# An RWKV block followed by a mixture of experts: the second product's weights copied into a tile with adjacent columns, the last routing groups reordered, row reads on two queues

## The chip, the core and the metric

The kernel runs on one core of a Trainium2 chip. A core has five engines that run side by side and meet through semaphores: TensorE (PE in the profile, its weight loads are PEld), VectorE (DVE), ScalarE (ACT), GpSimd (POOL) and SyncE (SP, which here only issues transfers). The metric is the device time of one execution in microseconds; lower is better. All data is float32.

## The reference, cut to what matters

```python
# attention: r, k, v of shape (4 batches, 8 heads, 768 steps, 48), decay w and bonus u per head
for t in range(S):
    cur  = einsum('bhd,bhe->bhde', u * k[t], v[t])
    y[t] = einsum('bhd,bhde->bhe', r[t], state + cur)
    state = w * state + einsum('bhd,bhe->bhde', k[t], v[t])
x = y rearranged to (3072 tokens, 384)

# mixture of experts: 4 groups x 4 experts, D = 384, F = 1024
g_idx = argmax(x @ w_group);            g_w = softmax(...)[g_idx]
e_idx = argmax(x @ w_expert[g_idx]);    e_w = softmax(...)[e_idx]
out[token] = g_w * e_w * (relu(x @ w1[g, e]) @ w2[g, e])
```

Each token goes to one of 16 experts. The two products `x @ w1` (384 by 1024) and `h @ w2` (1024 by 384) are the bulk of the arithmetic of the second half.

## The kernel before

The attention part works in chunks of 128 steps. As the tokens of a group of tiles are done, they are routed: logits, the choice of expert, a place in that expert's region of a buffer in device memory (`x_sorted`), and an indirect transfer (a scatter) that writes each row to its place. Then 17 items are worked through in turn. Items 0 and 1 both belong to the expert that is picked first (128 rows each); items 2 to 16 are one expert each, with 240, 233, 222, 216, 212, 206, 202, 199, 196, 193, 190, 187, 184, 178 and 173 rows.

```python
SLOTS = [256, 240, 233, 222, 216, 212, 206, 202, 199, 196, 193, 190, 187, 184, 178, 173]
ITEMS = [(0, 0, P), (0, P, SLOTS[0])] + [(e, 0, SLOTS[e]) for e in range(1, GE)]

# two places for an expert's weights, used in turn
places = [
    (wpool.tile([P, KO, F], FP32, name="w1"), wpool.tile([P, FO, DM], FP32, name="w2")),
    (kall..., rall...),            # the attention's tiles, used again
]

def up(i, f, beside=None):         # first product, two of eight blocks of 128 of F
    ...
    for q in range(2):
        if q == 1 and beside is not None:
            beside()
        for ko in range(KO):       # KO = 3
            nc.tensor.matmul(ph[:, q, :], lhsT=w1[:, ko, P * (f + q) : P * (f + q + 1)], rhs=xe[:, ko, 0:w], ...)
    nc.scalar.activation(hTs[i][:, f : f + 2, 0:w], ph, AF.Relu)

def down(i, d, beside=None):       # second product, one of three blocks d
    ...
    for fo in range(FO):           # FO = 8
        nc.tensor.matmul(
            po, lhsT=w2[:, fo].rearrange("p (c k) -> p k c", k=KO)[:, d], rhs=hT[:, fo, 0:w], ...
        )
    nc.scalar.copy(yo[i][:, d, 0:w], po)
```

A block `d` of the second product takes columns d, d + 3, d + 6, ... of `w2`: its weights lie 12 bytes apart in the tile. The rows come in with four transfers and a small one for the keys, are transposed by VectorE (`columns`), and leave by `pieces_out`: transposes, a multiplication by the gate, and scatters to the output.

```python
LAST = 5
for s in range(NT + LAST):         # NT = 24 tiles
    ...
    if s == FOUR * B + 10:         # s = 26
        columns(0)
    ...
    # rows_T(s - 4), row_logits(s - 5), back(s - 3), values(s - 2), scores(s - 1)
    if n in ROUTED:                # n = s - 5; the last groups are n = 21 and n = 23, two tiles each
        choice, before, gate, place, rows = routing(n)
        ...
    if s == FOUR * B + 10:
        up(0, 0)
up(0, 2)
placing = [part for _, part in todo.pop(NT + LAST)]
up(0, 4, placing[0])               # before() of the last group, between the two halves
for part in placing[1:]:           # gate(), place(), the scatters
    part()
up(0, 6)
load_rows(1, first, nc.sync)
... down(0, 0) ... down(0, 1); down(0, 2)
load_rows(2, second, nc.sync)
weights[1] = load_expert(second, 1)
...
columns(1)
pieces_out(0)
for i in range(1, len(ITEMS)):
    up(i, 0); up(i, 2)
    if i > 1: pieces_out(i - 1)
    up(i, 4); up(i, 6)
    if e < GE: load_rows(i + 2, expert, nc.sync)       # e = this expert + 2
    down(i, 0); columns(i + 1); down(i, 1); down(i, 2)
    if e < GE: weights[e] = load_expert(expert, e % 2)
```

Of the kernel before, what the change touches and what calls it, by code (L numbers as in the profile page):

```python
# [8 lines left out]
FP32 = mybir.dt.float32  # L9
# [25 lines left out]
def kernel(  # L35
# [313 lines left out]
    def route(pool, rb, xt, T, sums, number, group, apart=False):  # L349

        def tl(shape, name, dtype=FP32):
            return pool.tile(shape, dtype, tag=f"{name}_{T}", name=name)

        taken = [0]

        def part(k, pattern, **sizes):
            a = taken[0]  # L360
            taken[0] += T * k
            return rb[:, a : a + T * k].rearrange(pattern, i=T, **sizes)

        L = part(NL, "p (i a e) -> p i a e", e=Eg)
        key = part(NL, "p (i a e) -> p i a e", e=Eg)
        ohx = part(GE, "p (i g e) -> p i g e", e=Eg)
        ohp = part(GE, "p (i g e) -> p i g e", e=Eg)
        sx = part(NA, "p (i a) -> p i a")
        se = part(1, "p (i a) -> p i a")
        ohg = tl([P, T, Eg], "ohg")  # L370
        place_f = part(1, "p (i a) -> p i a")
        pre = bank([P, T, GE], "pre") if apart else part(GE, "p (i e) -> p i e")
        mx, kx = tl([P, T, NA], "mx"), tl([P, T, NA], "kx")
        ohe = tl([P, T, G, Eg], "ohe")
        ex = tl([P, T, NA, Eg], "ex")
        place_i = tl([P, T], "place_i", U32)

        def choice():
            nc.vector.reduce_max(out=mx, in_=L, axis=AX)

            nc.vector.tensor_tensor(out=key, in0=L, in1=spread(mx, 3, Eg), op=OP.is_ge)
            nc.vector.tensor_mul(
                key.rearrange("p i a e -> p (i a) e"), key.rearrange("p i a e -> p (i a) e"), spread(desc, 1, T * NA)
            )
            nc.vector.reduce_max(out=kx, in_=key, axis=AX)
            nc.vector.tensor_tensor(out=ohg, in0=key[:, :, 0, :], in1=spread(kx[:, :, 0], 2, Eg), op=OP.is_equal)
            nc.vector.tensor_tensor(out=ohx, in0=key[:, :, 1:NA, :], in1=spread(kx[:, :, 1:NA], 3, Eg), op=OP.is_equal)
            nc.vector.tensor_mul(ohe, ohx, spread(ohg, 3, Eg))
            nc.vector.tensor_mul(ohp, ohx, spread(ohg, 3, Eg))
            for i in range(T):  # L390
                nc.vector.tensor_add(sums[:, i + 1, :], sums[:, i, :], ohp[:, i].rearrange("p g e -> p (g e)"))
            nc.vector.tensor_sub(ex, L, spread(mx, 3, Eg))
            nc.scalar.activation(ex, ex, AF.Exp)

        def before():
            nc.tensor.matmul(
                pre.rearrange("p i e -> p (i e)"), lhsT=later, rhs=ohe.rearrange("p i g e -> p (i g e)"),
                start=True, stop=False,
            )
            nc.tensor.matmul(  # L400
                pre.rearrange("p i e -> p (i e)"), lhsT=ones, rhs=sums[:, 0:T, :].rearrange("p i e -> p (i e)"),
                start=False, stop=True,
            )

        def gate():
            nc.vector.reduce_sum(out=sx, in_=ex, axis=AX)
            gg = tl([P, T, G], "gg")
            nc.vector.scalar_tensor_tensor(
                out=gg, in0=sx[:, :, 1:NA], scalar=1e-9, in1=ohg, op0=OP.add, op1=OP.mult
            )  # L410
            ge = tl([P, T, 1], "ge")
            nc.vector.reduce_sum(out=ge, in_=gg, axis=AX)
            nc.vector.scalar_tensor_tensor(out=se, in0=sx[:, :, 0:1], scalar=1e-9, in1=ge, op0=OP.add, op1=OP.mult)
            nc.vector.reciprocal(xt[:, :, DM + ROW_GATE : DM + ROW_GATE + 1], se)
            nc.scalar.copy(xt[:, :, DM + ROW_ID], number)

        def place():
            at = tl([P, T, GE], "at")
            nc.vector.tensor_mul(at, pre, ohe.rearrange("p i g e -> p i (g e)"))
            nc.vector.reduce_sum(out=place_f, in_=at, axis=AX)  # L420
            nc.vector.tensor_copy(place_i, place_f.rearrange("p i a -> p (i a)"))

        def rows(i):

            ins = nc.gpsimd.indirect_dma_start(  # L425
                out=xs_dram, out_offset=bass.IndirectOffsetOnAxis(ap=place_i[:, i : i + 1], axis=0),
                in_=xt[:, i, :], in_offset=None, bounds_check=GE * RG - 1, oob_is_err=False,
            )
            tc.declare_no_dep(ins.ins, group=group, reason="no place is given twice")
            tc.add_to_no_dep_group(group, ins.ins)  # L430

        return choice, before, gate, place, rows

    places = [
        (wpool.tile([P, KO, F], FP32, name="w1"), wpool.tile([P, FO, DM], FP32, name="w2")),
# [2 lines left out]
            rall.rearrange("p j a h d -> p (j a h d)")[:, 0 : FO * DM].rearrange("p (k d) -> p k d", d=DM),  # L438
        ),
    ]  # L440

    def load_w1(e, i):
        for q in range(P // BL):
# [44 lines left out]
    def padded(n):  # L488
        return -(-n // BL) * BL

    def load_rows(i, expert, queue):

# [6 lines left out]
        xg, key = xgs[i] = tl([P, n // BL, KO, BL], "xg"), tl([P, n // BL, ROW_EXTRA], "key")  # L501
        a, w, rows = ITEMS[i][1], padded(width(i)), regions[bass.ds(expert, 1)]
        for q in range(P // BL):
            queue.dma_start(
                out=xg[BL * q : BL * (q + 1), 0 : w // BL].rearrange("t b k d -> t b (k d)"),
                in_=rows[:, a : a + w, BL * KO * q : BL * KO * (q + 1)].rearrange("a (b t) d -> t (a b) d", t=BL),
            )
        p = P if is_last(i) else BL
        n = -(-w // p) * p
        queue.dma_start(out=key[0:p, 0 : n // p], in_=rows[:, a : a + n, DM:XW].rearrange("a (j p) w -> p (a j) w", p=p))  # L510

    def columns(i):
        xg, key = xgs.pop(i)
        w = padded(width(i))
        xe = xes[i] = item_tile(i, [P, KO, room(i)], "xe")
        for ko in range(KO):
            nc.vector.transpose(xe[:, ko, 0:w].rearrange("p (b t) -> p b t", t=BL), xg[:, 0 : w // BL, ko, :])  # L517
        ids = item_tile(i, [P, room(i) // BL], "ids", U32, bufs=4)
        gates = item_tile(i, [P, room(i) // BL], "gates", bufs=4)
        if is_last(i):  # L520
# [16 lines left out]
    def up(i, f, beside=None):  # L537
# [13 lines left out]
                )  # L551
        nc.scalar.activation(hTs[i][:, f : f + 2, 0:w], ph, AF.Relu)  # L552

    def down(i, d, beside=None):

        w = width(i)
        if d == 0:
            yo[i] = item_tile(i, [P, KO, room(i)], "yo")
            if w < padded(w):
                nc.vector.memset(yo[i][:, :, w : padded(w)], 0.0)  # L560
        w2, hT = weights[ITEMS[i][0]][1], hTs[i]
        po = bank([P, w], "po")
        for fo in range(FO):
            if fo == FO // 2 and beside is not None:
                beside()
            nc.tensor.matmul(  # L566
                po, lhsT=w2[:, fo].rearrange("p (c k) -> p k c", k=KO)[:, d], rhs=hT[:, fo, 0:w], start=(fo == 0), stop=(fo == FO - 1)
            )
        nc.scalar.copy(yo[i][:, d, 0:w], po)  # L569

# [180 lines left out]
    def routing(n):  # L751
# [3 lines left out]
        b0 = b + 1 - T  # L755
        return route(
            rpool, lgs.pop(n), xts[c][:, b0 : b + 1, :], T, cum[:, first : n + 2, :], tok[:, c, b0 : b + 1],
            "rows to places", n == NT - 1,
        )

    scale_k(0, nc.vector, 0, 1)
# [9 lines left out]
            skip_runtime_bounds_check_because="four bits of a whole number",  # L771
        )

    LAST = 5
    for s in range(NT + LAST):
        pieces = todo.pop(s, [])

# [32 lines left out]
        n = s - 5  # L810
        if 0 <= n < NT:
            row_logits(n)
        if 0 <= s - 3 < NT:
            back(s - 3)
        if 0 <= s - 2 < NT:
# [21 lines left out]
            span_decay()  # L837
        if s == 4:
            check_decay()
        if n in ROUTED:  # L840
            choice, before, gate, place, rows = routing(n)
            T = ROUTED[n]
            if n >= NT - B - 1:
                choice()
                todo.setdefault(s + 1, []).extend(
                    [("last", part) for part in (before, gate, place)]
                    + [("last", lambda i=i, rows=rows: rows(i)) for i in range(T)]
                )
            else:
                todo.setdefault(s + 1, []).append(("choice", choice))  # L850
                todo.setdefault(s + 2, []).extend([("first", before), ("last", gate), ("last", place)])
                for i in range(T):
                    at = s + 3 + (0 if n == FOUR * B - 1 else i)
                    todo.setdefault(at, []).append(("last", lambda i=i, rows=rows: rows(i)))
        if s == FOUR * B + 10:
            up(0, 0)
    up(0, 2)
    placing = [part for _, part in todo.pop(NT + LAST)]
    up(0, 4, placing[0])
    for part in placing[1:]:  # L860
        part()
    up(0, 6)
    load_rows(1, first, nc.sync)

    left_i = cst([1, 1], "left_i", I32)
    keys = token_keys(NT)
# [25 lines left out]

    with ExitStack() as moe:
        pools[1] = moe.enter_context(tc.tile_pool(name="moe", bufs=2, reuse_waits="tile"))
        with tc.manual_schedule(engines={mybir.EngineType.PE}):
            columns(1)
            pieces_out(0)
            for i in range(1, len(ITEMS)):
                up(i, 0)
                up(i, 2)  # L900
# [8 lines left out]
                down(i, 0)  # L909
                if i + 1 < len(ITEMS):  # L910
                    columns(i + 1)
                down(i, 1)
                if i + 1 < len(ITEMS):
                    down(i, 2)
# [6 lines left out]
    with tc.If(more > 0, preferred_fallthrough_block=False):  # L921
        with tc.tile_pool(name="rest", bufs=1) as rest:
# [15 lines left out]
            with tc.If(ok < 1):  # L938
                with tc.tile_pool(name="scan", bufs=1) as sc:
# [54 lines left out]
                    with tc.For_i(0, NT, 1) as i:  # L994
# [7 lines left out]
                        rb = route_bank()  # L1002
                        logits(xT, rb[:, 0:NL])
                        again = route(sc, rb, xr, 1, cum[:, 0:2, :], number, "rows to places again")
                        for part in again[0:4]:
                            part()
                        again[4](0)
                        nc.vector.tensor_copy(cum[:, 0, :], cum[:, 1, :])
                        nc.vector.tensor_scalar(out=number, in0=number, scalar1=float(P), scalar2=None, op0=OP.add)
                    nc.vector.tensor_copy(cum[:, NT, :], cum[:, 0, :])  # L1010
# [136 lines left out]
```

## Time and profile before

| | |
|---|---|
| median of 3 runs | 452.63 us (451.78 to 452.81) |
| span of the profiled execution | 450.0 us, mean granted TensorE clock 0.994 |
| attention, routing, first product of item 0 | 0 to 164.41 us |
| second product of item 0, all of item 1 (128 rows each) | 164.41 to 190.03 us |
| items 2 to 16 | 190.03 us to the end |

A row of a group of instructions reads: line, engine, operation, output and inputs, shapes, count, then busy microseconds, mean nanoseconds of one, and the engine's idle time before them with what ended it. A float32 matmul of the program is two matmul instructions in the trace, so the 24 matmuls of one `up` or `down` block are 48 records. The mean time of one matmul record contains its way through the array; how often one can start is read from the starts of blocks in the order of time. In a table of stretches the granted clock is 1.00 for full speed, and the DMA share is the mean busy share of the 16 transfer engines (values a little over 1 occur in short stretches).

### The profile page before, as it was taken

What the parts mean: (1) busy time and instruction counts of PE and PEld (TensorE: products, weight loads), DVE (VectorE), ACT (ScalarE), POOL (GpSimd) and SP (SyncE); (2) the same over time, 40 slices, a digit from 0 to 9 for tenths busy, and PEclk for the clock granted to TensorE, in tenths of its full rate; (3) what the DMA queues carried; (4) which work ended last, traced back from release to release, by engine and by line L of the source; (5) the groups of instructions that cost most, each with busy time, mean ns of one, the idle gap of its engine ahead of it and who ended that gap; (6) DMA issues with size and microseconds to landing.
All of it is one profiled execution on the core that took longest, in us unless ns stands there. A gap on an engine that the chain in (4) does not pass through costs nothing. (4 is left out here: it accounts for less than half of the span.)

```text
span 450.0 us, 9430 instructions
## 1 busy us (share of the span) xinstructions
PE 432.0 (96%) x3463; PEld 419.5 (93%) x3463; DVE 186.9 (42%) x616; ACT 138.6 (31%) x418; POOL 198.7 (44%) x209
## 2 busy tenths in 40 slices
PE   6899999999999798999999999999999999999994
PEld 5698999999999698999999999999999999999993
DVE  6575678867795862223031230132133232121111
ACT  2884565556556321121121211211211211111110
POOL 7855536666653243031533623623632632442351
PEclk9999999999999998999999999999999999999999
DMA  9999999970116646998987989899998998989200
GB/s 175 239 253 197 263 272 210 212 143 37 37 38 164 202 147 153 269 263 181 276 222 167 249 231 198 233 242 205 248 247 181 260 252 179 271 230 232 73 23 29
DMA packets 126418, 86.65 MB, mean 193 GB/s; under 512 B 98982, under 2 KB 115509, under 8 KB 126364
## 3 DMA queue, kind: packets, MB, share of 16 engines
q1 hardware_dynamic: 115020, 69.18, 67.1%
q0 software_dynamic: 4960, 9.48, 7.0%
q10 hardware_dynamic: 6384, 7.31, 5.0%
q8 instruction: 29, 0.48, 0.5%
q14 instruction: 25, 0.20, 0.2%
HBM read 70.15 MB, written 16.44 MB: 192 GB/s over the span
## 5 line engine op out<-in xcount | busy, mean ns | idle before, releaser
L605 POOL DMA_INDIRECT out_dram<-yp,ids x104 | 101.0, 972 | 168.3 <-DVE yo L560 125.3
L598 DVE STREAM_TRANSPOSE yr<-yo 128x224 f32<-128x224 f32 (+3 forms) x48 | 22.2, 463 | 194.1 <-ACT yo L569 194.1
L566 PE MATMUL po<-hT,w 128*128 128x128 f32 (+7 forms) x432 | 78.3, 341 | 0.0
L566 PEld LDWEIGHTS po<-hT,w 128*128 128x128 f32 x432 | 77.5, 258 | 0.0
L548 PE MATMUL ph<-xe,w 128*128 128x128 f32 (+7 forms) x432 | 71.8, 327 | 2.3 <-DVE xe L517 1.6
L548 PEld LDWEIGHTS ph<-xe,w 128*128 128x128 f32 x432 | 69.9, 196 | 3.0 <-DVE xe L517 1.7
L566 PE MATMUL po<-hT,rall 128*128 128x240 f32 (+7 forms) x384 | 70.7, 344 | 0.0
L566 PEld LDWEIGHTS po<-hT,rall 128*128 128x128 f32 x384 | 69.9, 257 | 0.0
L548 PE MATMUL ph<-xe,kall 128*128 128x240 f32 (+7 forms) x384 | 67.0, 334 | 0.0
L548 PEld LDWEIGHTS ph<-xe,kall 128*128 128x128 f32 x384 | 65.3, 190 | 0.6
L552 ACT ACTIVATE hT<-ph 128x256 f32<-128x256 f32 (+15 forms) x68 | 33.5, 493 | 104.0 <-PE ph L548 104.0
L569 ACT COPY yo<-po 128x128 f32<-128x128 f32 (+15 forms) x51 | 16.3, 320 | 127.4 <-PE po L566 127.4
L648 ACT ACTIVATE dv<-vt,du 128x48 f32<-128x48 f32 x192 | 45.9, 325 | 1.9 <-DVE du L642 1.9
L425 POOL DMA_INDIRECT x_sorted<-xt,place_i x24 | 23.7, 989 | 25.0 <-DVE xe L517 12.9
L678 DVE TENSOR_TENSOR am<-pa,later 128x512 f32<-128x512 f32 x48 | 30.9, 685 | 8.9 <-PE pa L673 8.6
L637 POOL TENSOR_TENSOR dg<-rall,kall 128x768 f32<-128x768 f32 x12 | 21.9, 1823 | 24.7 <-DVE du L642 24.7
L632 POOL TENSOR_TENSOR kh<-kall,T 128x768 f32<-128x768 f32 (+1 forms) x12 | 21.6, 1800 | 19.2 <-DMA kall<-in_k_dram 17.6
L673 PE MATMUL pa<-rT,kT 48*128 48x128 f32 x384 | 28.4, 285 | 0.4 <-DVE rT L661 0.4
L695 PE MATMUL py<-am,vt 128*64 128x128 f32 x384 | 26.5, 279 | 0.0
L673 PEld LDWEIGHTS pa<-rT,kT 48*128 48x128 f32 x384 | 23.6, 187 | 2.2 <-DVE rT L661 0.6
L663 ACT COPY kT<-pk 128x512 f32<-128x512 f32 x24 | 14.0, 583 | 34.6 <-PE pk L659 27.0
L695 PEld LDWEIGHTS py<-am,vt 128*64 128x64 f32 x384 | 20.7, 136 | 3.2 <-issue 0.7
(139 smaller groups left out, 447.4 us busy)
## 6 DMA issues: line engine op xcount, KB each, us to landing
w<-in_moe_w_dram SPq DMA_DIRECT2D x32, 384.0 KB, 4.4
w<-in_moe_w_dram SPq DMA_DIRECT2D x8, 1536.0 KB, 8.3
kall<-in_moe_w_dram SPq DMA_DIRECT2D x32, 384.0 KB, 6.7
rall<-in_moe_w_dram SPq DMA_DIRECT2D x8, 1536.0 KB
x_sorted<-nothing ACTq DMA_DIRECT2D x4, 1544.0 KB, 8.0
rall<-in_r_dram SPq DMA_DIRECT2D x12, 384.0 KB
vt<-in_v_dram SPq DMA_DIRECT2D x12, 384.0 KB, 7.4
kall<-in_k_dram SPq DMA_DIRECT2D x10, 384.0 KB, 6.1
```

The lines of the kernel that those rows point to most:

```text
L425: ins = nc.gpsimd.indirect_dma_start(out=xs_dram, out_offset=bass.IndirectOffsetOnAxis(ap=place_i[:, i : i + 1], axis=0), in_=xt[:, i, :], ...
L548: nc.tensor.matmul(ph[:, q, :], lhsT=w1[:, ko, P * (f + q) : P * (f + q + 1)], rhs=xe[:, ko, 0:w], start=(ko == 0), stop=(ko == KO - 1), s ...
L552: nc.scalar.activation(hTs[i][:, f : f + 2, 0:w], ph, AF.Relu)
L566: nc.tensor.matmul(po, lhsT=w2[:, fo].rearrange("p (c k) -> p k c", k=KO)[:, d], rhs=hT[:, fo, 0:w], start=(fo == 0), stop=(fo == FO - 1))
L598: nc.vector.transpose(yr[:, 0:b, :, d], y[:, d, 0:w].rearrange("p (b t) -> p b t", t=BL))
L605: ins = nc.gpsimd.indirect_dma_start(out=out_pieces, out_offset=bass.IndirectOffsetOnAxis(ap=ids[:, j : j + 1], axis=0), in_=yp[:, j], in_ ...
L632: engine.tensor_mul(khs[g % (RING - 1)][:, a0:a1, :, 0:D], kts[g % RING][:, a0:a1], spread(T2[m], 1, a1 - a0))
L637: nc.gpsimd.tensor_mul(dg, rts[g % RING][:, :, :, 0:D], kts[g % RING])
L648: nc.scalar.mul(dv[:, h, :], vts[g % (RING + 1)][:, a, h, 0:D], dvs[g][:, a, h : h + 1])
L673: nc.tensor.matmul(pa[e][:, hc, :], lhsT=kT[rows, hc, :], rhs=rT[rows, hc, :], start=True, stop=True, skip_group_check=True,)
L678: nc.vector.tensor_mul(am[:, e], pa[e], spread(later, 1, HP))
L695: nc.tensor.matmul(py[DP * e : DP * (e + 1), hc, :], lhsT=vt[:, a, 2 * hc + e, :], rhs=am[:, e, hc, :], start=(c == 0), stop=True, skip_gr ...
```

## The change

ScalarE copies `w2` of the item into a new tile `w2_parts` in which the 128 columns of a block d are adjacent, two of the eight row blocks per copy, four copies per expert; `down` takes its weights from there. The original tile is free for the next transfer once it has been copied. Of the last two routing groups, the last is chosen one step earlier, in the last loop step rather than one after it, and with the matmuls of `up(0, 2)` ahead of its logits. The exponentials of the routing become a part of their own, the keys of item 0 are worked on later, and VectorE's order in the expert loop is now the program's, with item 1's columns ahead of item 0's output. The four row reads of item 1 are issued in turn by SyncE and ScalarE.

```diff
+    w2_parts = wpool.tile([P, FO, KO, P], FP32, name="w2_parts")
 ...
         nc.scalar.activation(hTs[i][:, f : f + 2, 0:w], ph, AF.Relu)
 
+        behind = {2: (0,), 4: (2,), 6: (4, 6)} if i > 1 else {4: (0, 2), 6: (4, 6)}
+        if i != 1:
+            w2 = weights[ITEMS[i][0]][1]
+            for a in behind.get(f, ()):
+                nc.scalar.copy(w2_parts[:, a : a + 2], w2[:, a : a + 2, :].rearrange("p f (c k) -> p f k c", k=KO))
 ...  (down)
-                po, lhsT=w2[:, fo].rearrange("p (c k) -> p k c", k=KO)[:, d], rhs=hT[:, fo, 0:w], ...
+                po, lhsT=w2_parts[:, fo, d, :], rhs=hT[:, fo, 0:w], ...
 ...  (load_rows)
+            if other is not None and q % 2:
+                of, by = regions[bass.ds(other[0], 1)], other[1]
+            else:
+                of, by = rows, queue
+            by.dma_start(
 ...  (routing: exponentials and row numbers a part of their own)
+        def exps():
             nc.scalar.activation(ex, ex, AF.Exp)
+            nc.scalar.copy(xt[:, :, DM + ROW_ID], number)
 ...
-    LAST = 5
+    LAST = 4
     for s in range(NT + LAST):
 ...
+        if s == NT + LAST - 1:
+            up(0, 2)
+            row_logits(NT - 1)
 ...
-        if n in ROUTED:
-            choice, before, gate, place, rows = routing(n)
+        for n in (n, NT - 1) if s == NT + LAST - 1 else (n,):
+            if n not in ROUTED:
+                continue
+            choice, exps, before, gate, place, rows = routing(n)
 ...
-    up(0, 2)
-    placing = [part for _, part in todo.pop(NT + LAST)]
-    up(0, 4, placing[0])
-    for part in placing[1:]:
+    exps, before, *placing = [part for _, part in todo.pop(NT + LAST)]
+    exps()
+    up(0, 4, before)
+    for part in placing:
         part()
     up(0, 6)
-    load_rows(1, first, nc.sync)
+    load_rows(1, first, nc.sync, (expert_of(first_i[0:1, 0:1], (mybir.EngineType.Activation,)), nc.scalar))
 ...
-        with tc.manual_schedule(engines={mybir.EngineType.PE}):
+        with tc.manual_schedule(engines={mybir.EngineType.PE, mybir.EngineType.DVE}):
             columns(1)
+            keys_in(0)
             pieces_out(0)
+            keys_in(1)
```

## The prediction

> **What bounds the kernel now.** I read the page first. TensorE and its weight loads are busy nearly throughout; the other engines are under half. The chain that ended last is of no use here: it holds one scatter of 0.91 us at the very end. So the question is what sets TensorE's pace. The groups of instructions, shapes apart, give it:
>
> ```profile
> PE 432.0 (96%) x3463; PEld 419.5 (93%) x3463; DVE 186.9 (42%) x616; ACT 138.6 (31%) x418; POOL 198.7 (44%) x209
> ...
> L566 PEld LDWEIGHTS po<-hT,w 128*128 128x128 f32 x432 | 77.5, 258 | 0.0
> ...
> L548 PEld LDWEIGHTS ph<-xe,w 128*128 128x128 f32 x432 | 69.9, 196 | 3.0 <-DVE xe L517 1.7 <-PE pb L729 1.0
> ```
>
> Both load 128 columns, but the second product (L566), whose columns lie 12 bytes apart, takes 258 ns where the first (L548), with adjacent ones, takes 196. Loads overlap matmuls, so that hurts only where the load and not the moving rows sets the pace. TensorE's order in time, each block 48 records, shows where:
>
> ```profile
> 281.07 8.52 PE L548 MATMUL ph<-xe,w 128*128 128x206 f32 x48
> 289.44 8.53 PE L566 MATMUL po<-hT,w 128*128 128x206 f32 x48
> ...
> 411.33 7.40 PE L548 MATMUL ph<-xe,w 128*128 128x178 f32 x48
> 418.57 8.53 PE L566 MATMUL po<-hT,w 128*128 128x178 f32 x48
> 426.94 7.20 PE L548 MATMUL ph<-xe,kall 128*128 128x173 f32 x48
> ```
>
> From start to start, the first product's block shrinks with the rows: 8.37 us at 206, 7.24 us at 178. The second product's stays at 8.36 to 8.39 us for every width from 206 down (289.44 to 297.80; 418.57 to 426.94). That is 8.37 / 48 = 174 ns per record: the pace of a strided load. Above 206 rows the two blocks are equal, and the moving rows bind.
>
> Last, the order in time between item 0 and item 1, and the granted clock there:
>
> ```profile
> 168.93 1.85 SPq L504 DMA_DIRECT2D xg<-x_sorted  x4
> ...
> 173.06 0.27 ACT L569 COPY yo<-po 128x128 f32<-128x128 f32 x1 [2.56 <-PE po L566]
> ...
> 173.74 0.56 DVE L600 TENSOR_TENSOR yp<-yr,gates 128x384 f32<-128x384 f32 x1
> 174.22 0.69 DVE L517 STREAM_TRANSPOSE xe<-xg 128x128 f32<-128x128 f32 x3
> 174.57 7.25 PE L548 MATMUL ph<-xe,w 128*128 128x128 f32 x48 [1.55 <-DVE xe L517]
> 181.66 8.53 PE L566 MATMUL po<-hT,w 128*128 128x128 f32 x48
> ```
>
> ```profile
> 174.00:176.00 2.00, 1.43 (x7) 1.43 (x8) 1.96 (x12) 0.00 (x0) 1.12 (x2) 0.70 0.67 152
> 176.00:178.00 2.00, 2.00 (x12) 2.00 (x11) 0.14 (x2) 0.38 (x1) 1.70 (x2) 0.50 1.09 246
> ```
>
> In the second (the stretch, then busy time of TensorE, its loads, VectorE, ScalarE and GpSimd, then granted clock, DMA share, GB/s) the clock falls. VectorE makes item 1's columns only after item 0's output (yp), which waits for the end of item 0's second product. TensorE stands 1.55 us, and then runs at clock 0.50: item 1's first product takes 181.66 - 174.57 = 7.09 us. Its last two pairs, by the starts of the relus after them (179.18, 180.52, 181.86), take 1.34 us each at full clock, so a warm block is 4 x 1.34 = 5.4 us.
>
> **What the Trainium skill says.** "TensorE: Matmul & The Clock Gate", section "LDWEIGHTS (loading the stationary operand)", puts a load at P / 1.2 ns, 107 ns for 128 columns. Adjacent columns agree: 1.34 us / 12 = 112 ns per record at 128 rows. The strided loads at 174 ns do not. "SBUF — State Buffer", section "Door 1: The DMA port swizzle", gives a reason: SBUF lines are 16 bytes, and each crossing to a new line costs. At a step of 12 bytes three of four columns begin a new line. The trace shows the slow load, not its cause. "ScalarE: Activation LUTs", section "What ACT_TABLE_LOAD costs", puts an operation with immediates at 186 + 0.833 N ns: a copy of 768 elements is about 0.83 us, an estimate; whether strided reads slow ScalarE too is not said. The first page, "What's actually happening", halves the clock after an idle window of about 3.4 us; the half clock above lasts about that long.
>
> **The change part by part.**
>
> *Adjacent columns, items 7 to 16.* The second product's block should take what the first product's takes at the same width. With 8.37 us before in each case, the first product's starts give 8.20, 8.08, 7.96, 7.84, 7.72, 7.60, 7.48, 7.24 and 7.04 us for 202, 199, 196, 193, 190, 187, 184, 178 and 173 rows. The gains are 0.19 + 0.30 + 0.43 + 0.53 + 0.65 + 0.78 + 0.89 + 1.13 + 1.33 = 6.2 us, all on the path, because TensorE waits for nothing from 190 us to the end but 0.4 us in the last turn. Items 2 to 6 gain nothing.
>
> *Item 1* has 128 rows: 8.37 - 5.4 = 3.0 us, on the path. It needs no copies; item 0's serve.
>
> *The copies.* Four per expert, 64 in all, about 53 us of ScalarE at 0.83 us; in the expert loop it now uses about 3 of each 16 us. By the built order of ScalarE's instructions, all four stand ahead of the last relu for items 2 to 16. Take 173 rows, where time is shortest, and a pessimistic 1.23 us per copy (strided reads slowed as the loads are: 768 x 1.36 + 186 ns). Pairs of the first product come every 1.76 us. Relu, one copy, relu end at 4.2 us; two copies 6.7; relu 7.1; copy 8.4; relu 8.8. The second product starts at 7.0 and wants the last relu at its seventh step, 7.0 + 12 x 0.147 = 8.8 us. It just fits; at 0.83 us it fits with room. So the copies cost TensorE nothing in these items.
>
> *Item 0* is different: two copies stand ahead of its last relu and two behind, with pairs only 1.34 us apart. Counting from the old times: relu of the third pair at 163.8, copies to 165.5, relu 165.9, copies to 167.6. TensorE's first block d starts at about 165 and waits at its fifth and seventh steps until then, ends near 168, and two blocks of 1.8 us end at about 171.7 (pessimistic copies: 173.2). Before, it ended at 172.8. Of the 3 us that faster loads give item 0, most goes to waiting for copies.
>
> *Routing.* Item 0's keys out of the way save VectorE 1.1 us ahead of the second-last choice (153.96 to 155.07). But its exponentials now stand on ScalarE behind the relu of `up(0, 2)`, about 158.3, where they ran at 157.80. The gate and place chains follow each other as before. I find the last scatter issued at about 164.8, as before: no gain, and TensorE stands some 2 us at 160 to 162 for the last choice, with a risk to its clock.
>
> *Row reads and columns.* Issued on two queues, the four reads take 0.9 instead of 1.85 us from 168.93, land 1.8 us later (the median of issues of this size) at about 171.7, and VectorE is free: columns by 172.4. Item 1 then starts when item 0 ends, at about 172.9 instead of 174.57: 1.7 us. With no long stand, most of the 1.7 us lost to the half clock (7.09 - 5.4) returns; I take 1.0.
>
> Sum: 6.2 + 3.0 + 1.7 + 1.0 = 11.9 us; less 0.5 us for transfers that come late at the start (below): 11.4. 452.63 - 11.4 = 441.2 us.
>
> **The rivals.**
>
> *Transfers become the bound.* Expert 1's weights are issued at 174.09 and the transfers are full from about 176 to 204 (columns as above):
>
> ```profile
> 190.03:209.47 19.44, 19.44 (x97) 18.85 (x97) 4.11 (x16) 3.27 (x7) 3.88 (x4) 1.00 1.00 223
> 395.48:411.33 15.85, 15.85 (x97) 15.85 (x97) 3.86 (x16) 2.85 (x7) 5.84 (x6) 1.00 0.93 235
> ```
>
> TensorE reaches item 2 about 6 us earlier. Its w1, last issued at 175.6 with 6.6 us to landing (182.2), would be in time for about 183.8, its w2 near 188, before the copies hold anything up. Later an item needs 0.93 x 15.85 = 14.7 us of transfers against a shortest new cycle of 15.2 us while weights are still loading, and the early release of w2 starts them some 6 us sooner. It fits, narrowly. If not, 3 to 5 us are lost: 445.
>
> *ScalarE becomes the bound*, if a strided copy takes over 1.3 us: each item's second product then waits for relus and copies, up to 1 us in the narrow ones, and the gain there is gone: 449 to 452.
>
> *The clock.* The stand at 160 to 162 and the waits in item 0 put item 0 and 1 at half clock; 2 to 4 us of the transition are lost: 444.
>
> *The transition gains nothing, the rest holds*: 6.2 + 3.0 = 9.2 us, 443.4.
>
> **Range and chances.** The 9.2 us rest on blocks measured in this trace; the 2.7 us of the transition and clock are sequenced by hand. The 2% mark is 443.6, only 2.4 us above my figure, and any one rival crosses it. I take 437.5 to 446, and 0.72 faster, 0.25 within 2%, 0.03 slower.
>
> **What would show it.** Right: second-product blocks of the same length as first-product blocks at every width; weight loads of both products near 190 to 196 ns; copies of 0.8 to 1.2 us; no wait of TensorE after 190 us; item 1 starting near 173 at full clock. Wrong: TensorE waiting on ScalarE in the blocks of L585 beyond item 0, on transfers of items 2 to 4, or blocks of the second product still at 8.37 us, which would mean that the stride does not set the pace.

## The result, and the profile after

| | before | after |
|---|---|---|
| median (4 runs each) | 452.72 us (451.78 to 452.84) | 439.76 us (439.21 to 440.08) |
| span of the profiled execution | 450.0 us | 438.3 us |
| mean granted TensorE clock | 0.994 | 0.993 |

The ratio is 0.9717, with a 95% interval of 0.9700 to 0.9734: faster by 2.8%. 441.2 us had been predicted.

On the page of the changed kernel, the engines' totals and the groups that answer to those shown of before (line, engine, operation, tiles, count, then busy us, mean ns of one, and the idle time before them):

```profile
PE 420.7 (96%) x3463; PEld 406.4 (93%) x3463; DVE 187.6 (43%) x616; ACT 208.1 (47%) x482; POOL 198.8 (45%) x209
...
L585 PEld LDWEIGHTS po<-hT,w_parts 128*128 128x128 f32 x816 | 133.5, 191 | 3.6 <-ACT hT L565 1.8
...
L561 PEld LDWEIGHTS ph<-xe,w 128*128 128x128 f32 x432 | 69.5, 194 | 1.3 <-PE pb L748 1.0
...
L571 ACT COPY w_parts<-rall 128x768 f32<-128x768 f32 x32 | 38.1, 1239 | 4.0 <-DMA rall<-in_moe_w_dram 4.0
L571 ACT COPY w_parts<-w 128x768 f32<-128x768 f32 x32 | 37.9, 1236 | 0.4 <-DMA w<-in_moe_w_dram 0.4
```

The loads of the second product now take 191 ns, where they took 258, and are level with those of the first. The price stands in the last two lines: 64 copies of 1.24 us, 76 us together. They overlap other instructions a little: ScalarE's busy time rose by 69.5 us, from 138.6 to 208.1. The copies also waited once for 4.0 us on a transfer; that comes back below.

TensorE in order of time at the same widths as before (start, busy us, line, operation, tiles, shape, records):

```profile
275.72 8.52 PE L561 MATMUL ph<-xe,w 128*128 128x206 f32 x48
284.08 8.52 PE L585 MATMUL po<-hT,w_parts 128*128 128x206 f32 x48
...
402.20 7.40 PE L561 MATMUL ph<-xe,w 128*128 128x178 f32 x48
409.44 7.40 PE L585 MATMUL po<-hT,w_parts 128*128 128x178 f32 x48
416.68 7.20 PE L561 MATMUL ph<-xe,kall 128*128 128x173 f32 x48
```

Both blocks are now equal at 178 rows: 7.24 us from start to start (402.20 to 409.44, 409.44 to 416.68). Before, the second took 8.37 us there. At 206 rows nothing changed, 8.36 us. No bracket with a wait stands behind any of these records.

The change from item 0 to item 1, with the row reads and columns of item 1, same view over all engines:

```profile
168.73 0.83 SPq L513 DMA_DIRECT2D xg<-x_sorted  x2
168.91 0.90 ACTq L513 DMA_DIRECT2D xg<-x_sorted  x2
...
171.84 0.70 DVE L526 STREAM_TRANSPOSE xe<-xg 128x128 f32<-128x128 f32 x3 [3.54 <-DMA xg<-x_sorted]
...
172.31 5.53 PE L561 MATMUL ph<-xe,w 128*128 128x128 f32 x48
177.67 5.52 PE L585 MATMUL po<-hT,w_parts 128*128 128x128 f32 x48
```

Item 1 starts at 172.31 us instead of 174.57, without a wait, and both of its blocks take 5.36 us (172.31 to 177.67 to 183.03) instead of 7.09 and 8.37.

By stage, from starts of blocks in both traces. These are the starts of items 3 and 8 before, and of item 8 after (that of item 3 after is shown below):

```profile
209.47 9.60 PE L548 MATMUL ph<-xe,w 128*128 128x233 f32 x48
...
297.80 8.36 PE L548 MATMUL ph<-xe,kall 128*128 128x202 f32 x48
```

```profile
292.44 8.36 PE L561 MATMUL ph<-xe,kall 128*128 128x202 f32 x48
```

| stage | before | after | gain | gain predicted |
|---|---|---|---|---|
| up to the start of item 1 | 174.57 | 172.31 | 2.26 | 1.7 |
| item 1, first product | 7.09 | 5.36 | 1.73 | 1.0 |
| item 1, second product | 8.37 | 5.36 | 3.01 | 3.0 |
| item 2 | 19.44 | 21.09 | -1.65 | -0.5 |
| items 3 to 7 | 88.33 | 88.32 | 0.01 | 0 |
| items 8 to 16 and the end | 152.20 | 145.86 | 6.34 | 6.2 |
| sum | 450.0 | 438.3 | 11.7 | 11.4 |

(The prediction counts items 7 to 16 together; item 7, with 206 rows, had no gain to give.) The medians differ by 12.96 us and these two executions by 11.64 (451.72 and 440.08), so about 1.3 us of the difference lies in which executions were profiled.

The one stage that lost is item 2. First TensorE there, then ScalarE, in order of time:

```profile
183.03 9.96 PE L561 MATMUL ph<-xe,kall 128*128 128x240 f32 x48
192.83 0.97 PE L585 MATMUL po<-hT,w_parts 128*128 128x240 f32 x4
194.34 1.08 PE L585 MATMUL po<-hT,w_parts 128*128 128x240 f32 x4 [0.54 <-ACT hT L565]
195.92 8.37 PE L585 MATMUL po<-hT,w_parts 128*128 128x240 f32 x40 [0.51 <-ACT hT L565]
204.12 9.60 PE L561 MATMUL ph<-xe,w 128*128 128x233 f32 x48
```

```profile
185.74 0.57 ACT L565 ACTIVATE hT<-ph 128x480 f32<-128x480 f32 x1 [2.24 <-PE ph L561]
190.30 3.52 ACT L571 COPY w_parts<-rall 128x768 f32<-128x768 f32 x3 [3.99 <-DMA rall<-in_moe_w_dram]
193.73 0.56 ACT L565 ACTIVATE hT<-ph 128x480 f32<-128x480 f32 x1
194.19 1.21 ACT L571 COPY w_parts<-rall 128x768 f32<-128x768 f32 x1
195.31 1.01 ACT L565 ACTIVATE hT<-ph 128x480 f32<-128x480 f32 x2
```

A wait of ScalarE for a transfer has become a wait of TensorE for relus. ScalarE had done the relu of item 2's first pair at 186.3 us and next has copies, whose source, expert 1's `w2` (`rall`), landed only at about 190.3, 15.3 us after its issue at 174.97. The relus of the later pairs stand behind the copies in ScalarE's order, so TensorE, which never reads `rall`, stands in its second product for `hT`. That block takes 11.29 us (192.83 to 204.12) instead of 9.71 before (199.76 to 209.47), 1.05 of it in the two waits shown.

Last, a stand of TensorE in item 0, and the granted clock after it (stretch, then busy us of TensorE, its loads, VectorE, ScalarE and GpSimd, then clock, DMA share, GB/s):

```profile
161.42 0.38 PE L399 MATMUL pre<-ohe,later 128*128 128x32 f32 x2 [1.94 <-DVE rb L389]
```

```profile
162.00:164.00 2.00, 2.00 (x14) 2.00 (x14) 1.31 (x8) 1.31 (x4) 0.82 (x1) 0.64 0.55 200
164.00:166.00 2.00, 2.00 (x11) 2.00 (x11) 0.22 (x2) 2.00 (x4) 1.20 (x2) 0.51 0.03 6
```

The half clock has not gone. In the trace before it lay in item 1 (from about 175 to 178 us); here it lies in item 0, behind a stand of TensorE of 1.94 us for the last routing choice, which the kernel before did not have.

### The profile page after: what moved, and what is told of

Its sections match the earlier page's. It is cut to its first block, busy times and chain, and to the rows that moved or that the text cites. A ratio compares the mean times of both kernels' runs of the same rounds, so it can differ in the third digit from the quotient of the medians.

```text
span 438.3 us, 9515 instructions
## 1 busy us (share of the span) xinstructions
PE 420.7 (96%) x3463; PEld 406.4 (93%) x3463; DVE 187.6 (43%) x616; ACT 208.1 (47%) x482; POOL 198.8 (45%) x209
## 5 line engine op out<-in xcount | busy, mean ns | idle before, releaser
L585 PE MATMUL po<-hT,w_parts 128*128 128x128 f32 (+15 forms) x816 | 138.0, 328 | 1.6 <-ACT hT L565 1.0
L585 PEld LDWEIGHTS po<-hT,w_parts 128*128 128x128 f32 x816 | 133.5, 191 | 3.6 <-ACT hT L565 1.8
L561 PEld LDWEIGHTS ph<-xe,w 128*128 128x128 f32 x432 | 69.5, 194 | 1.3 <-PE pb L748 1.0
L571 ACT COPY w_parts<-rall 128x768 f32<-128x768 f32 x32 | 38.1, 1239 | 4.0 <-DMA rall<-in_moe_w_dram 4.0
L571 ACT COPY w_parts<-w 128x768 f32<-128x768 f32 x32 | 37.9, 1236 | 0.4 <-DMA w<-in_moe_w_dram 0.4
```

The lines of the kernel that those rows point to most:

```text
L571: nc.scalar.copy(w2_parts[:, a : a + 2], w2[:, a : a + 2, :].rearrange("p f (c k) -> p f k c", k=KO))
L585: nc.tensor.matmul(po, lhsT=w2_parts[:, fo, d, :], rhs=hT[:, fo, 0:w], start=(fo == 0), stop=(fo == FO - 1))
```

## The experiments

The theory: the second product's pace up to 206 rows is set by how fast weights are read at a step of 12 bytes; the copies remove that, and nearly all of the gain is theirs. The rivals: the gain comes from the order of the last routing groups, the columns and the two queues; or the copies put a price of their own on ScalarE that eats part of it.

The experiments ran on three chips. The runs with other steps, with VectorE's old order and with adjacent columns ran on the first, where the kernel before took 453.35 us. The other experiments ran on two chips on which ScalarE stands for several microseconds at places where the first chip's traces show next to nothing (the kernel before took 466.75 us on one, called the most disturbed below, and 454.80 on the other), so that of these only ratios on one chip, and blocks without a wait in them, are read. Times on different chips are compared by their ratios to the kernel before on the same chip (0.9717 for the change).

### The change without its copies

```diff
-            for a in behind.get(f, ()):
-                nc.scalar.copy(w2_parts[:, a : a + 2], w2[:, a : a + 2, :].rearrange(...))
-                po, lhsT=w2_parts[:, fo, d, :], rhs=hT[:, fo, 0:w], ...
+                po, lhsT=w2[:, fo].rearrange("p (c k) -> p k c", k=KO)[:, d], rhs=hT[:, fo, 0:w], ...
```

> The changed kernel without the copies: the second product takes its weights 12 bytes apart again, everything else stays changed. Theory (the step of the loads sets the pace where rows are few): blocks of the second product of 8.37 us for 128 rows and for every width from 206 down, so items 1 and 7 to 16 give back 3.0 + 6.3 us, item 0 ends 0.7 us later, item 2 loses its wait of 1.6 us: 439.8 + 3.0 + 6.3 + 0.7 - 1.6 = 448.2 us. Rival (routing, order and queues carry most of the gain): 442 to 444 us.

> The changed kernel without the copies, again, as the chip of the first run was disturbed (the kernel before took 460 to 476 us there). As before: 448.2 us if the step of the loads carries the gain, with item 1 and items 7 to 16 back at 8.37 us per block of the second product; 442 to 444 us if routing, order and queues carry it. On the disturbed chip ScalarE's last relu of an item came late in 10 items; if that belongs to this kernel and not to the chip, it is seen here too, 460 us or more.

On the most disturbed chip 476.01 us, 1.0226 of before (1.0152 to 1.0300); again on another, 457.10 us against 454.80, 1.0064 (1.0029 to 1.0098). So without the copies nothing is gained on these chips, and a little is lost. TensorE of the second of these, in order of time:

```profile
416.73 7.40 PE L560 MATMUL ph<-xe,w 128*128 128x178 f32 x48
423.97 8.53 PE L579 MATMUL po<-hT,w 128*128 128x178 f32 x48
432.34 7.20 PE L560 MATMUL ph<-xe,kall 128*128 128x173 f32 x48
```

The second product's block is back at 8.37 us (423.97 to 432.34) beside a first of 7.24, with everything else of the change in place: it is the strided read that holds it. The size of the loss is not a clean number. ScalarE shows stands such as this one, in the same trace:

```profile
310.26 0.51 ACT L564 ACTIVATE hT<-ph 128x404 f32<-128x404 f32 x1 [3.75 <-remote]
```

This is the last relu of an item, late by some 2 us. TensorE waits for it with 0.86 us in that block; in the first run 46.3 us of ScalarE's idle time ended so, at 13 relus, and TensorE waited 15.2 us behind 10 of them. "Remote" here names no work on this core that ended the wait. What these stands wait for was not found.

### The copies without the rest of the change

```diff
 (before)
+    w2_parts = wpool.tile([P, FO, KO, P], FP32, name="w2_parts")
 ...  behind the relus in up(), as in the change
+            for a in behind.get(f, ()):
+                nc.scalar.copy(w2_parts[:, a : a + 2], w2[:, a : a + 2, :].rearrange("p f (c k) -> p f k c", k=KO))
 ...
-                po, lhsT=w2[:, fo].rearrange("p (c k) -> p k c", k=KO)[:, d], rhs=hT[:, fo, 0:w], ...
+                po, lhsT=w2_parts[:, fo, d, :], rhs=hT[:, fo, 0:w], ...
```

> The kernel before with the copies alone: old routing, one queue, old order of VectorE. Theory: 452.7 - 9.3 - 0.5 (item 0 a little shorter) + 0.8 (item 2 waits for its weights) = 443.7 us, item 1 starting near 174 at half clock. Rival (routing, order and queues carry most): 448 us or more.

> The kernel before with the copies alone, again, for the same reason. Theory: 443.7 us, item 1 starting near 174.5 at half clock, item 2 without a wait because it starts some 4 us later than in the changed kernel and its weights have landed by then. Rival (routing, order and queues carry most of the gain): 448 us or more.

457.18 us, 0.9813 of before (0.9726 to 0.9900), on the most disturbed chip; 448.25 us, 0.9868 (0.9828 to 0.9907), on the other. On that other chip copies alone gain 6.5 us where the rest of the change alone lost 2.3. By the ratio, 452.72 us would become 446.7, between the 443.7 of the theory and the 448 of the rival; 2.44 us of it are a wait of TensorE in item 3 for a relu behind one of ScalarE's stands. TensorE there:

```profile
409.51 7.40 PE L550 MATMUL ph<-xe,w 128*128 128x178 f32 x48
416.75 7.40 PE L574 MATMUL po<-hT,w_parts 128*128 128x178 f32 x48
```

7.24 us each, as in the change. The trace also shows what the rest of the change is there to repair: item 1's first product waits 1.55 us for its columns again, as in the kernel before, and item 0's second product waits three times for copies (0.40, 0.77 and 0.27 us). Item 1 then runs at full clock, 5.47 us (176.97 to 182.44), where the half clock had been expected. Item 2 waits for nothing, as expected.

### Weights at steps of 1 to 8 floats

If the step sets the load's pace, other steps must give other paces. The change without copies reads, in seven items, the weights of each block at a step of its own; the outputs of these items are products with other columns of `w2`, at the same amount of work.

```diff
+        STEPS = {0: (4, 6, 8), 1: (1, 2, 3), 12: (1, 2, 3), 13: (4, 6, 8), 14: (1, 2, 3), 15: (4, 5, 6), 16: (1, 2, 4)}
+        step = STEPS.get(i, (3, 3, 3))[d]
+        flat = w2.rearrange("p f d -> p (f d)")
 ...
+            return flat[:, o : o + P * step].rearrange("p (c k) -> p k c", k=step)[:, 0]
```

> No copies; in items 0, 1 and 12 to 16 the three blocks of the second product read their 128 columns at other steps: 4, 6, 8 elements (item 0), 1, 2, 3 (items 1, 12, 14), 4, 6, 8 (13), 4, 5, 6 (15), 1, 2, 4 (16). Those items compute with other weights than the reference. Lines theory (each new 16-byte line costs): pace grows with the share of columns on a new line, 1/4, 1/2, 3/4, 1: step 1 at 112 ns (at 128 rows), step 2 between 112 and 145, step 3 174, step 4 near 205, and 5, 6, 8 the same as 4. Rival (any step but 1 costs the same, 174 ns). Rival (pace grows on with the step): 8 above 4.

The time was 455.67 us in one run. A block d has 16 records and ends with ScalarE's copy `yo`; from one such copy to the next is one block. ScalarE in order of time, item 1 (steps 1, 2, 3 at 128 rows), then item 13 (steps 4, 6, 8 at 187 rows):

```profile
184.56 0.27 ACT L592 COPY yo<-po 128x128 f32<-128x128 f32 x1 [1.40 <-PE po L589]
186.48 0.27 ACT L592 COPY yo<-po 128x128 f32<-128x128 f32 x1 [1.65 <-PE po L589]
189.30 0.27 ACT L592 COPY yo<-po 128x128 f32<-128x128 f32 x1 [2.56 <-PE po L589]
...
393.27 0.32 ACT L592 COPY yo<-po 128x187 f32<-128x187 f32 x1 [3.26 <-PE po L589]
397.11 0.32 ACT L592 COPY yo<-po 128x187 f32<-128x187 f32 x1 [3.52 <-PE po L589]
```

Step 2 takes (186.48 - 184.56) / 16 = 120 ns per record, step 3 (189.30 - 186.48) / 16 = 176, step 8 (397.11 - 393.27) / 16 = 240. With the other items: 112 ns at step 1 (blocks of 128 rows in the change), 220 at 5, 223 at 6, and about 234 at 4 (less sure, as it was first of its item each time and had to be read from the start of the item). So it is not a matter of adjacent or not: step 2 is nearly free, step 3 costs half as much again, from step 4 the pace stays at about twice, above the 205 ns expected. That follows the share of columns that begin a new line of 16 bytes, 1/4, 1/2, 3/4 and then 1 of them. Both rivals fall: step 2 is far below 174 ns, and steps 5 and 6 lie below step 4, so the pace does not just grow with the step.

### Copies at steps of 1, 2 and 4 floats

```diff
+                step = {3: 1, 4: 1, 5: 2, 6: 2, 7: 4, 8: 4, 9: 1, 10: 1, 11: 2, 12: 4}.get(i, 3)
 ...
+                    nc.scalar.copy(out_parts, flat[:, o : o + 2 * DM * step].rearrange("p (c k) -> p k c", k=step)[:, 0])
```

The copies of items 3 to 12 take other elements of `w2`, as many and into the same tile.

> The changed kernel, but the copies of items 3, 4, 9, 10 read adjacent elements, those of 5, 6, 11 every second, those of 7, 8, 12 every fourth; the rest as before, every third. Those items then multiply by other weights than the reference. Lines theory (ScalarE's read of SBUF pays for new lines as TensorE's does): adjacent near 0.83 us, every second about 0.83 to 1.05, every third 1.24, every fourth about 1.45 us. Rival (ScalarE's own cost for this copy is 1.24 us whatever the step).

The time was 440.57 us in one run. One line's instructions by stretches, steps 1, 2 and 4 (count, then min/median/max ns, first and last start, shapes), and then the line with the copies at step 3:

```profile
L578 ACT COPY w_parts<-w x4: 822/828/833, 311.3 to 314.0; 128x768 f32<-128x768 f32 x4
...
L578 ACT COPY w_parts<-w x4: 882/887/909, 343.3 to 346.1; 128x768 f32<-128x768 f32 x4
...
L578 ACT COPY w_parts<-rall x4: 1572/1576/1588, 359.0 to 363.8; 128x768 f32<-128x768 f32 x4
```

```profile
L574 ACT COPY w_parts<-w x12: 1205/1240/1259, 163.4 to 408.7; 128x768 f32<-128x768 f32 x12
```

ScalarE pays the same toll as the weight loads, and step 4, at 1.58 us, more than the 1.45 expected. Each further float of the step, up to four, lets another quarter of the elements begin a new line: 192 of a copy's 768, 32 of a load's 128. From step 2 to 3 and from 3 to 4 a copy grows by 353 and 336 ns, which is 1.84 and 1.75 ns per new line. A load takes 120, 176 and about 234 ns for its 64, 96 and 128 lines, 1.88, 1.83 and 1.83 ns per line. At step 2 the lines have only just overtaken the pace of adjacent elements: 120 against 112 ns for a load, 887 against 828 for a copy. The Trainium skill ("Advanced Engine Details and Errata", section "SBUF Cachelines") asks for at least two hits on a line to hide the memory's latency: step 2, with just two, comes within 7% of full pace in both engines.

One line of that trace bears on the rival in which ScalarE becomes the bound: at 190 rows and 1.58 us per copy, TensorE waits in the second product for a relu, 0.23 us, and the block takes 8.22 us where the change has 7.72. At 1.24 us no item from 3 on waits for a relu or a copy.

### VectorE's old order for item 1

```diff
-            columns(1)
             keys_in(0)
             pieces_out(0)
+            columns(1)
             keys_in(1)
```

> The changed kernel with VectorE's old order at item 1: item 0's output before item 1's columns. Theory (the order is what lets item 1 start early): item 1 starts after item 0's end, its yo, three transposes and the product, about 173.7 instead of 172.3, perhaps at half clock: 441.2 us, up to 442.9 with the half clock. Rival (the row reads, not the order, bind): 439.8 to 440.2 us.

440.80 us (440.25 to 441.45), 0.9728 of before (0.9708 to 0.9747), against 0.9717 (0.9700 to 0.9734) for the change: no difference is shown by the times. TensorE:

```profile
175.12 5.62 PE L561 MATMUL ph<-xe,w 128*128 128x128 f32 x48 [1.55 <-DVE xe L526]
...
195.66 9.88 PE L585 MATMUL po<-hT,w_parts 128*128 128x240 f32 x48
205.38 9.60 PE L561 MATMUL ph<-xe,w 128*128 128x233 f32 x48
```

Not all of the later start is the order's doing. The end of item 0 (its last `yo`) here and in the change, and the granted clock here:

```profile
173.60 0.27 ACT L588 COPY yo<-po 128x128 f32<-128x128 f32 x1 [1.52 <-PE po L585]
```

```profile
172.51 0.27 ACT L588 COPY yo<-po 128x128 f32<-128x128 f32 x1 [1.52 <-PE po L585]
```

```profile
162.00:164.00 2.00, 2.00 (x10) 2.00 (x11) 1.33 (x9) 0.32 (x2) 0.94 (x1) 0.50 0.54 195
...
166.00:168.00 2.00, 2.00 (x11) 2.00 (x11) 0.97 (x6) 2.00 (x3) 0.86 (x1) 0.50 0.52 198
```

Item 1 starts 2.81 us later than in the change (175.12 against 172.31). Of this, 1.09 us come from item 0, which ends later because the half clock holds until about 168 us here and until 166 in the change, behind the same stand and before the two programs differ. The order's own part is the other 1.72 us. Yet item 3 starts only 1.26 us later (205.38 against 204.12), because item 2's second product takes 9.72 us (195.66 to 205.38) and waits for nothing. Expert 1's `w2` lands as before: its copies start at 190.24 us here and at 190.30 in the change, and the transfer engines are full from 176 us on in both. So in this stretch an earlier TensorE meets a transfer that doesn't come earlier. Less the 1.09 us of the clock, about 0.2 us of the 1.72 would be left at item 3 (an estimate from these starts): nearly all that the columns' new place gains is handed back at item 2.

### Adjacent columns without copies

The change without its copies, and the second product taking columns 128 d to 128 d + 127 of `w2`; the output columns come out in another order, at the same work.

```diff
-                po, lhsT=w2[:, fo].rearrange("p (c k) -> p k c", k=KO)[:, d], rhs=hT[:, fo, 0:w], ...
+                po, lhsT=w2[:, fo, P * d : P * (d + 1)], rhs=hT[:, fo, 0:w], ...
```

> No copies; block d of the second product is columns 128 d to 128 d + 127 of w2, adjacent without a copy, so the output columns come in another order than the reference's. Shows what the copies cost beside TensorE. Theory (they cost item 2's wait and a part of item 0's, nothing else): 438.2 us, blocks of items 3 to 16 as in the changed kernel. Rival (ScalarE's copies also slow TensorE, by access to SBUF or by late relus): 436 us or less.

439.22 us (438.81 to 440.18), 0.9699 of before (0.9675 to 0.9723), no worse than the change's 0.9717. The kernel without copies in the first experiment differs from this one in the step of the weights alone, and stood at 1.0064 and 1.0226 on the other chips. So the gain is there with no copy at all: adjacency brings it, and the copies are only its price. In TensorE's order of time:

```profile
165.35 6.42 PE L579 MATMUL po<-hT,w 128*128 128x128 f32 x48
172.82 5.63 PE L560 MATMUL ph<-xe,w 128*128 128x128 f32 x48 [1.05 <-DVE xe L525]
```

Item 0's second product no longer waits for copies, but item 1 then waits 1.05 us for its columns: here the reads, issued 0.5 us later than in the change, end the transition. Item 2's second product takes 9.72 us instead of 11.29. Together item 3 starts at 203.09 us against 204.12, so the copies cost the change 1.0 us by the traces. From there to the end both kernels take 234.2 us, so the copies slow TensorE nowhere else: the rival falls.

### Items left without copies

```diff
-        if i != 1:
+        if i != 1 and not 2 <= i <= 2:      (second kernel: 2 <= i <= 6)
 ...  down(): in these items weights from w2 at its step of three, as before
```

Items 2 to 6 have 212 rows and more, where the strided load is hidden.

> The changed kernel, but item 2 (240 rows) takes its weights strided from the transfer's tile and has no copies. Theory (item 2's second product waited because its w2 landed late and the copies stood ahead of the relus): its second product goes from 11.29 to 9.71 us and TensorE waits no more there: 438.2 us. Rival (the transfers are simply late, and the wait moves on to item 3): 439.8 us.

> The changed kernel with no copies for items 2 to 6 (240 to 212 rows), which take their weights strided. Theory (a strided load hides behind 206 or more moving rows): as with item 2 alone, 438.2 us, blocks of items 2 to 6 unchanged. Rival (w2's tile comes free later, so the transfers of items 4 to 8 land late): 440 us or more, with waits for transfers.

> The changed kernel with no copies for items 2 to 6, again. Theory (item 2 waited for copies of weights that landed late; a strided load hides behind 206 rows or more): 438.2 us, item 2's second product 9.7 instead of 11.3 us, blocks of items 2 to 6 as in the changed kernel. Rival (w2's tile comes free later and later transfers are late): 440 us or more, with TensorE waiting for transfers or ScalarE waiting for w2 from item 4 on.

464.01 us (0.9973, 0.9938 to 1.0008) and 465.90 us (0.9937, 0.9882 to 0.9992) on the most disturbed chip, where before spread from 460 to 476: no comparison with the change can be drawn from them. The second again, on the other chip: 448.47 us, 0.9874 (0.9831 to 0.9916). In its trace the strided blocks of items 5 and 6, undisturbed, take 8.76 and 8.60 us, as with copies, and ScalarE and TensorE wait for no transfer from item 2 on: the rival's late transfers are not there. Item 2's second product takes 9.72 us (197.27 to 206.99) without a wait, but that proves nothing here: starting that late it takes 9.72 us with copies too, as in VectorE's old order, where it starts at 195.66. What the copies do at item 2 is shown by the kernel with adjacent columns, not by these. Whether they beat the change in time stays open; by these blocks about 438.2 us could be expected on a chip without the stands (an estimate: 439.76 less 1.6). No run here is a shown improvement on the change.

### The old order of the last routing groups

```diff
-    LAST = 4
+    LAST = 5
 ...
-        if s == NT + LAST - 1:
-            up(0, 2)
-            row_logits(NT - 1)
 ...  up(0, 2) after the loop, as before
```

> The changed kernel with the old order of the last routing groups (one loop step more, the product of item 0 after it); copies, order of VectorE and the two queues stay. Theory (the new order gains nothing, because the exponentials moved behind a relu): 439.6 to 440.1 us, the last scatter within 0.3 us of 164.5. Rival (it gains the 1.1 us that VectorE saves): 440.9 us or more, last scatter near 165.6.

445.31 us, 0.9794 (0.9765 to 0.9822), the best ratio on that chip; the change itself did not run there. The last two scatters issue at 165.93 and 167.21 us, against 166.72 and 167.99, and 167.69 and 168.96, in the two runs with the new order on that chip. All scatters come later on that chip, so the first of the last two is better counted from the scatter three before it: 6.38 us here, 7.27 and 8.55 in those two, 6.54 in the change and 6.86 in the kernel before. The old order is thus no slower than the change's, and the 1.1 us of the rival are not there. A cost of the new order isn't shown either. In the two late runs the second-last group's exponentials stand directly behind the relu of `up(0, 2)` (159.85 and 160.93 us), and that relu is late for other reasons: in one, ScalarE began it 0.8 us after TensorE had gone on to the next product, against 0.2 in the change; in the other, TensorE ran at half clock from 156 to 158 us. The two queues were not varied by themselves.

## Why the prediction was right

*Items 7 to 16, 6.2 us, and item 1's second product, 3.0 us.* Measured 6.34 and 3.01. The step that carries them, taking the second product's block to be as long as the first's at the same width, held at every width. The copies, which bring back adjacency, are shown to be what does it, and adjacency without copies does the same.

*The copies.* 0.83 us was the estimate from the fixed and per-element cost; they took 1.24. The other estimate, 768 x 1.36 + 186 ns = 1.23 us, which carried the pace of the strided load over to ScalarE, was right to the hundredth. The conclusion drawn under it, that all fits behind the matmuls even at 173 rows, held: from item 3 on TensorE waits for nothing but 0.4 us in the last turn.

*Item 0.* It ended at 172.31 us, between the 171.7 and the 173.2 given for fast and slow copies. It waited twice for copies, 0.18 and 0.41 us, and ran at half clock besides; the columns came at 171.84 to 172.54 us, so little of this was left to lose. The hand count began too late: the third pair's relu came at 162.94 us and not at 163.8, which made up for the slower copies.

*Routing.* No gain, as put: the scatters moved by 0.3 us. VectorE did begin the second-last choice 1.1 us earlier (154.43 against 155.57), and the exponentials behind the relu of `up(0, 2)` ran at 158.01, later than before (157.80).

*Row reads and columns, 1.7 us.* 2.26: item 1 started 0.6 us ahead of the 172.9 given, since item 0 ended that much sooner; the columns came as put (by 172.4 predicted, 172.54 measured).

*The half clock, 1.0 us.* The term was mis-sized: 1.73, all of what was lost in item 1. Nor is its mechanism shown. The prediction let the half clock go because the stand of 1.55 us goes. In three traces with that stand back (VectorE's old order, and both of the copies alone), item 1's first product ran at full clock all the same, in 5.46 to 5.47 us. That the trace before had the half clock there may be chance. The risk named for the stand at 160 to 162 us did come true, but it fell on item 0.

*Late transfers, 0.5 us.* The other mis-sized term, 1.65, and the one place where a sentence of the prediction failed: "its w2 near 188, before the copies hold anything up". `w2` landed at 190.3 us, and the copies held up the relus. The prediction had named this rival and put 3 to 5 us on it if it took hold throughout; it took hold in one item. The transition's and the clock's surplus (0.56 + 0.73) nearly cancel this shortfall (1.15), so that the traces' 11.7 us come so near the 11.4 predicted is in part luck.

*The rivals.* ScalarE did not become the bound; the run with 1.58 us copies shows that the edge lies between 1.24 and 1.58 us per copy at 190 rows, which has the 1.3 us in it that was named for the narrow items. "The transition gains nothing" fell: 3.99 us of the trace's gain are there, of which 1.65 are handed back in item 2. Of these, 1.72 are shown to be VectorE's order (at the start of item 1); the rest was not isolated.

## What to carry to other kernels

Where weight loads set a matmul's pace, look at the step of the weights in bytes: for float32, a step of two costs next to nothing and a step of three half as much again. So a copy pays where the moving rows are too few to hide the load (here from 202 rows down), and another order of columns pays without a copy, where the reader of the output can take it. When a copy is put between a transfer and its user, it stands in the order of an engine that others wait for: a late transfer that nobody needed yet then stops the relus behind the copy. And an engine that is made earlier gains only as far as the next transfer comes earlier too: look at when the transfer engines are full before counting an early start.

## What the runs showed of the hardware

- One toll for two engines: about 1.8 ns for each new 16-byte line, in the weight loads of TensorE (120 ns at step 2, 176 at step 3) and in ScalarE's copies (887, 1240 and 1576 ns at steps 2, 3 and 4) alike, and hidden, but for some 7%, when only half of the elements begin one. That both read by lines is the simplest account of the steps tried; the small spread from step 4 on (220 to 240 ns per record) it does not explain.
- The same stand need not give the same clock. The kernel before stood 1.55 us before item 1 and then ran at 0.50 for 3.4 us; the run with VectorE's old order stood 1.55 us at the same place and ran at 1.00. Behind the stand of 1.93 to 1.94 us in item 0 the half clock lasted 3.4 us in the change and in the kernel with adjacent columns, but 6.8 in the run with VectorE's old order (there the mean clock is 0.87, 0.50, 0.50, 0.50 and 0.92 in the stretches of 2 us from 160 us on, which makes 0.5 + 6 + 0.3 us at half). The Trainium skill ("TensorE: Matmul & The Clock Gate", section "What's actually happening") has a free-running window of activity of about 3.4 us, and says that the same kernel varies with where the window falls. These lengths agree with it, but the traces don't show the window. The section also puts an idle window of that length ahead of the half clock; here the stands ahead of it were only 1.55 and 1.94 us.
- On two of three chips ScalarE sat idle for 2 to 5 us at some relus and copies with no releaser on the core, in every trace taken there; the traces of the first chip hold one such stand, of 1.8 us. The cause stays open.
